# One pool of four PSUM banks for scores and shared tiles, single-bank refill, and another order of the last units in a fused attention and gated-feed-forward kernel

## The chip, the cores and the metric

The kernel runs on one core of a Trainium2 chip. Five engines work side by side, each in its own program order, and wait for one another through semaphores: PE (TensorE, matmuls), ACT (ScalarE), DVE (VectorE), POOL (GpSimd) and SP (SyncE, which issues the transfers). Matmuls write to eight accumulation banks of 128 x 512 fp32, called `ps` here. The metric is device time in microseconds (us), the median of several runs.

## The reference, cut to what matters

```
xn  = layernorm(x)                               # x: 1 x 2048 x 512, no scale, no shift
q, k, v = split(xn @ wqkv)                       # 32 heads of width 16
p   = softmax(q k^T / 4)                         # 2048 x 2048 per head
A   = (p v) @ wo
B   = (silu(xn @ w1) * (xn @ w3)) @ w2           # inner width 1792
out = x + A + B
```

Nearly all work of the attention is one element per score: 32 x 2048 x 2048 scores that are formed, whose row maximum is subtracted, that go through the exponential, and that meet v.

## The kernel before, in words

The heads are taken in 8 groups of four (one head on 32 rows of the PE array), the queries in 4 chunks of 512. A chunk and a group give two **units** of 256 queries; the last pair gives three, of 256, 128 and 128, so there are 65 units.

Each unit forms its scores twice. **Stage 1** (`p1_cand`, matmul L772) lays 128 queries against 512 keys for two heads into two banks; DVE takes the row maximum of both (L793, 128x1024), and when all of a unit's are there, L834 joins them into `negm`, the negated maximum. There are 1024 such steps, on bank pairs 0-1 and 2-3 in turn. POOL writes the negated maximum into `Z` (L810, L812); it reaches two spare rows of `QT` by two transfers, or, for the first unit and the last three (FAST_AUG), by a new projection of the queries with `Z` added (`tile_QT2`, evacuated by ACT at L602). **Stage 2** (`p2_cand`, matmul L888) then forms the transposed scores less the maximum, 512 columns (a bank) at a time, and ACT takes the exponential straight out of the bank (L905). There are 2048 such exponentials, in banks 4, 5 and 6 in a fixed rotation: number n goes to bank 4 + n mod 3.

Everything else shares **bank 7**, one tile at a time: the projections KT, QT and V, the product of weights and v (`tile_PV`, evacuated as `U` at L969), the feed-forward's gate and up tiles (L641, L643, L647), and the output tiles (L704). At the end the feed-forward part of the last outputs is set aside (`tile_OUTA`, L716), and once the last unit's attention is there, `tile_OUTB` adds the attention part (L729) in banks 0 to 3. All of these are column matmuls issued by one helper, L453. The last three units (FAST_PV) get their softmax sum by extra matmuls against ones, and DVE divides (L958, L960); the others go through a chain of transfers and POOL (L992, L1014).

The order of all instructions is fixed when the kernel is built. A planner keeps its own estimate of when each engine is free, and again and again emits the earliest candidate. `pick_pe` weighs three candidates for PE: a stage-1 step (a), a stage-2 step (b), a column matmul (c). Where there is no column matmul to do, `fill_cand` offers a **fill**: four matmuls of the identity against xnT into a free bank, whose result nobody reads (in the profile `ps<-xnT,ident`). It does so where the columns that the planner counted in the last `LOAD_WIN` = 2.3 us are under `LOAD_MIN` = 12000, between the 48th stage-1 step and the last one. `assign` gives banks to tiles; `choose` says which tile is next; `pv_ready` lets a PV tile start when at most 6 of its unit's exponentials are still to be emitted.

Of the kernel before, what the change touches and what calls it, by code (L numbers as in the profile page):

```python
# [225 lines left out]
def _build(nc, A_x, A_wqkv, A_wo, B_w1, B_w3, B_w2, out):  # L226
# [15 lines left out]
    STARVE = 0.7  # L242
    COUP = 0.1
    PACE = 4500
    PACE_CAP = 6000
    LAG = 44
    LOAD_WIN = 2.3
    LOAD_MIN = 12000

    units = []  # L250
    for qc in range(NQC):
# [4 lines left out]
    NU = len(units)  # L256
# [4 lines left out]
    P = _Prog()  # L261
# [4 lines left out]
    with ctx:  # L266
# [342 lines left out]
        def ffn_from(sc, fc):  # L609
            last = sc == NQC - 1  # L610
            lo = sc * CHUNK + (100 if sc else 40)
            hi = (sc + 1) * CHUNK + (-24 if last else LAG)
            return lo + (hi - lo) * fc // FC

        def ffn_pair(sc, fc):
# [230 lines left out]
        p2_n = [0]  # L846
        exp_n = [0]
        exp_unit = [0] * NU
        pt_free = list(range(NT, NPT))
        pt_slot = {}  # L850
        exp_emitted = set()

        def p2_cand():
# [1 line left out]
            if u >= NU or ("AUG", u) not in done or not pt_free:  # L855
                return None
            n = p2_n[0]
            if exp_n[0] < n - 2:
                return None
            b = 4 + n % 3  # L860
            if b in bank_tenant:
                return None
            qc, g, q0, nq = units[u]
            kpb = 512 // nq
# [17 lines left out]
            def emit():  # L882
                rest.pop(best[1])
                pt_free.pop(0)

                def f(e):
                    for i in range(kpb):
                        ins = e.matmul(bank(b)[:, i * nq:(i + 1) * nq],  # L888
                                       KT[32 * j:32 * j + 32, g, (k0 + i) * 128:(k0 + i + 1) * 128],
                                       QT[32 * j:32 * j + 32, qs, q0:q0 + nq],  # L890
                                       start=True, stop=True, tile_position=(32 * j, 0))
                    return ins
                P.pe(f, reads, writes, "row", (j,), kpb * _c_mm(nq), name="p2_%d" % n, first="act")
                note_load(st, 512)
                p2_n[0] += 1
                pt_slot[(u, kb, j)] = sl
                if not rest:
                    p2_u[0] += 1
                    p2_units_done[0] = p2_u[0]

                def cb(op):
                    exp_n[0] += 1
                    exp_unit[u] += 1
                    exp_emitted.add((u, kb, j))
                expq.append(_Item(lambda e: e.activation(PT[:, sl, :], bank(b), ACTF.Exp, scale=SCALE),  # L905
                                  [("ps", b)], [("PT", sl)], _c_act(512), cb=cb))
# [137 lines left out]
        def pv_ready():  # L1044
            u = pv_u[0]
            if u >= NU:
                return False
            left = len(p2_list[u]) - exp_unit[u]
            if left > 6:
                return False  # L1050
            if u in FAST_PV:
                return True
            return u < NUB or u_live[0] < NUB
# [29 lines left out]
        def assign():  # L1083
            if head_tiles or not (0 in pvlog or ("AUG", 0) in done):
                for bk in (7, 6, 5, 4):
                    if bk in bank_tenant or (bk != 7 and p2_n[0] > 0):
                        continue
                    for k, t in enumerate(head_tiles):
                        if ok(t):
                            give(head_tiles.pop(k), bk)  # L1090
                            break
            if 7 not in bank_tenant and not head_tiles:
                t = choose()
                if t is not None:
                    give(t, 7)
            if ("AUG", 0) not in done and p1_n[0] > 0 and not head_tiles:
                for bk in (6, 5, 4):
                    if bk not in bank_tenant and p2_n[0] == 0:
                        if crit and ok(crit[0]):
                            give(crit.pop(0), bk)  # L1100
            if red_n[0] >= NP1:
                for bk in (0, 1, 2, 3):
                    if bk not in bank_tenant and tail_outs and ok(tail_outs[0]):
                        give(tail_outs.pop(0), bk)
        pvlog = set()

        def col_cand():
            best = None
            for t in active:
                if not t.groups:  # L1110
                    continue
                g = t.groups[0]
# [37 lines left out]
            return st, emit, dur  # L1150

        couple = [-1.0]
        loadlog = []

        def note_load(st, w):
# [5 lines left out]
            return sum(w for t, w in loadlog if t >= st - LOAD_WIN) < LOAD_MIN  # L1161

        def fill_cand():
            if head_tiles or p1_n[0] < 48 or p1_n[0] >= NP1 or not low_load(P.free["pe"]):
                return None
            st = None
            for fb in (7, 4 + p2_n[0] % 3):
                if fb in bank_tenant or (fb != 7 and (exp_n[0] < p2_n[0] - 2 or p2_n[0] == 0)):
                    continue
                s_ = P.pe_start("col", None, P.ready("pe", (), [("ps", fb)]))  # L1170
                if st is None or s_ < st - 0.05:
# [10 lines left out]
            return st, emit, _c_mm(512)  # L1182
        n_fill = [0]

        def pick_pe():
            a = p1_cand()
            b = p2_cand()
# [6 lines left out]
                a[1]()  # L1194
            if b is not None and b[0] <= couple[0] + 0.12:
                return b[0], b[1]
            if c is None:
                if a is not None and (b is None or a[0] <= b[0] + COUP):
                    return a[0], go_a
                return None if b is None else (b[0], b[1])  # L1200
            if a is not None and a[2] <= end + 0.02:
                return a[0], go_a
            starving = (b is not None and b[2] <= max(end, c[0]) + 0.02 and not expq
                        and P.free["act"] < b[0] + STARVE)
            if a is None or c[0] + c[2] <= a[2] + TOL:
                if starving:
                    return b[0], b[1]
# [163 lines left out]
```

## Time and profile before

| what | value |
|---|---|
| median of 3 runs | 1308.74 us (1305.94 to 1310.98) |
| profiled execution: its time, its span | 1309.81 us, 1308.0 us |
| granted PE clock, mean over the span | 0.967 |
| busy: ACT, DVE, PE | 1223.6, 1199.7, 1194.0 us |
| 1024 row maxima on DVE (L793) | 1175.8 us busy |
| 2048 exponentials on ACT (L905) | 1084.4 us busy |
| fills on PE | 1528 matmuls, 131.0 us |
| the last row maximum ends | 1224.2 us |
| the last exponential ends | 1301.9 us |

The time is taken outside the program, the span from the first to the last instruction of the profiled execution. A busy engine is not always at its best pace: an instruction that comes alone is counted with its whole duration, while one that follows closely on another overlaps with it. So the mean spacing within a run of equal instructions tells more than the share of busy time.

### The profile page before, as it was taken

What the parts mean: (1) busy time and instruction counts of PE and PEld (TensorE: products, weight loads), DVE (VectorE), ACT (ScalarE), POOL (GpSimd) and SP (SyncE); (2) the same over time, 40 slices, a digit from 0 to 9 for tenths busy, and PEclk for the clock granted to TensorE, in tenths of its full rate; (3) what the DMA queues carried; (4) which work ended last, traced back from release to release, by engine and by line L of the source; (5) the groups of instructions that cost most, each with busy time, mean ns of one, the idle gap of its engine ahead of it and who ended that gap; (6) DMA issues with size and microseconds to landing.
All of it is one profiled execution on the core that took longest, in us unless ns stands there. A gap on an engine that the chain in (4) does not pass through costs nothing.

```text
span 1308.0 us, 39060 instructions
## 1 busy us (share of the span) xinstructions
PE 1194.0 (91%) x16785; PEld 439.0 (34%) x16785; DVE 1199.7 (92%) x1141; ACT 1223.6 (94%) x2413; POOL 357.6 (27%) x453
## 2 busy tenths in 40 slices
PE   5999899889999999999999999999999988899997
PEld 2323333333333333333333333333333333333334
DVE  6889999999999999999999999999999999999402
ACT  5689999999999999999999999999999999999984
POOL 4012332222321233323331133333331143443110
PEclk8979999999899999899999999999999999999985
DMA  7001100101010111111101111111101121110000
GB/s 217 3 14 24 27 18 17 25 18 25 18 21 22 34 26 25 25 26 27 25 16 27 34 27 24 25 26 27 23 18 27 23 44 33 35 24 9 5 5 18
DMA packets 112844, 36.24 MB, mean 28 GB/s; under 512 B 98232, under 2 KB 112672, under 8 KB 112672
## 3 DMA queue, kind: packets, MB, share of 16 engines
q1 hardware_dynamic: 112672, 33.76, 12.0%
q8 instruction: 131, 2.15, 0.7%
q14 instruction: 41, 0.34, 0.1%
HBM read 22.81 MB, written 2.10 MB: 19 GB/s over the span
## 4 chain that ended last, share of the span: by engine, by line
PE 52%; ACT 40%; DVE 4%; issue 2%; DMA 1%; SPq 0%
ACT PT L905 30%; PE ps L453 28%; PE ps L888 15%; PE ps L772 8%; DVE part L793 4%; ACT th L641 2%; ACT zg L643 2%; ACT ub L647 2%; ACT U L969 1%; ACT KT L536 1%; ACT QT L579 1%; DMA hT<-in_A_wqkv_dram 1%; ACT osb L704 0%; ACT osb L491 0%; DVE R L958 0%
## 5 line engine op out<-in xcount | busy, mean ns | idle before, releaser
L793 DVE TENSOR_REDUCE part<-ps 128x2 f32<-128x1024 f32 x1024 | 1175.8, 1216 | 28.6 <-PE ps L772 17.0
L905 ACT ACTIVATE PT<-ps 128x512 bf16<-128x512 f32 x2048 | 1084.4, 619 | 50.5 <-PE ps L888 34.2
L888 PE MATMUL ps<-QT,KT 32*128 32x256 bf16 (+1 forms) x4160 | 577.7, 276 | 20.6 <-ACT PT L905 9.6
L772 PE MATMUL ps<-KT,QT 32*128 32x512 bf16 x2048 | 444.4, 387 | 5.2 <-DVE part L793 4.3
L888 PEld LDWEIGHTS ps<-QT,KT 32*128 32x128 bf16 x4160 | 188.6, 93 | 312.6 <-ACT PT L905 235.2
L992 POOL TENSOR_TENSOR Rc<-Lc,mone 128x8 f32<-128x8 f32 x62 | 101.5, 1637 | 390.6 <-DMA Lc<-U 390.6
L453 PE MATMUL ps<-PT,Vaug 128*17 128x256 bf16 (+1 forms) x4160 | 178.8, 279 | 14.1 <-ACT zg L643 2.4
L453 PE MATMUL ps<-xnT,w 128*32 128x512 bf16 x1792 | 142.0, 390 | 32.9 <-ACT zg L643 22.5
L772 PEld LDWEIGHTS ps<-KT,QT 32*128 32x128 bf16 x2048 | 114.8, 91 | 160.6 <-issue 96.6
L453 PE MATMUL ps<-xnT,ident 128*32 128x512 bf16 x1528 | 131.0, 391 | 2.4
L453 PEld LDWEIGHTS ps<-PT,Vaug 128*17 128x17 bf16 x4160 | 83.2, 91 | 98.4 <-issue 60.6
L628 POOL TENSOR_TENSOR a<-zg,ub 128x512 f32<-128x512 bf16 x56 | 64.7, 1155 | 126.1 <-ACT ub L647 126.1
L810 POOL TENSOR_SCALAR Z<-negm 128x8 bf16<-128x8 f32 x64 | 14.7, 229 | 210.2 <-DVE negm L834 210.2
L630 POOL TENSOR_TENSOR hT<-a,t 128x512 bf16<-128x512 f32 x56 | 71.1, 1270 | 3.1
L453 PEld LDWEIGHTS ps<-xnT,w 128*32 128x32 bf16 x1792 | 37.1, 95 | 98.8 <-issue 83.1
L453 PE MATMUL ps<-w,hT 128*32 128x512 bf16 x896 | 70.3, 384 | 0.0
L958 DVE RECIPROCAL R<-ps 128x128 f32<-128x128 f32 (+1 forms) x3 | 3.7, 1224 | 71.3 <-PE ps L453 71.3
L453 PEld LDWEIGHTS ps<-xnT,ident 128*32 128x32 bf16 x1528 | 31.1, 94 | 59.0 <-issue 39.1
L453 PE MATMUL ps<-xnT,wk_on 128*32 128x512 bf16 x512 | 42.2, 406 | 7.0 <-ACT KT L536 4.9
L626 POOL TENSOR_SCALAR t<-th 128x512 f32<-128x512 bf16 x56 | 34.9, 623 | 49.9 <-ACT th L641 49.8
L453 PE MATMUL ps<-xnT,wq 128*32 128x512 bf16 (+2 forms) x576 | 41.8, 369 | 7.2 <-ACT U L969 2.5
L1014 POOL TENSOR_TENSOR on_b<-U,R 128x256 bf16<-128x256 f32 x32 | 23.3, 728 | 56.6 <-DMA R<-Rrow 56.6
(75 smaller groups left out, 458.7 us busy)
## 6 DMA issues: line engine op xcount, KB each, us to landing
w<-in_B_w_dram SPq DMA_DIRECT2D x112, 128.0 KB
R<-Rrow SPq DMA_DIRECT2D x248, 16.0 KB
PT<-in_A_x_dram SPq DMA_DIRECT2D x4, 512.0 KB
xr<-in_A_x_dram SPq DMA_DIRECT2D x16, 128.0 KB
out_dram<-osb SPq DMA_DIRECT2D x16, 128.0 KB
QT<-Zs SPq DMA_DIRECT2D x122, 2.0 KB
w<-in_B_w_dram SPq DMA_DIRECT2D x1, 1792.0 KB
hT<-in_A_wqkv_dram SPq DMA_DIRECT2D x3, 512.0 KB
```

The lines of the kernel that those rows point to most:

```text
L453: ins = e.matmul(bank(bk)[32 * i:32 * i + m, c0:c0 + ncols], make_lhsT(i), rhs_ap(i), start=start, stop=stop, tile_position=(0, 32 * i), **kw)
L626: q.append(_Item(lambda e: e.tensor_scalar(t1[:, :], th[:, ss, :], 1.0, 1.0, ALU.mult, ALU.add), [("th", ss)], [("t1",)], 0.62, 0.72))
L628: q.append(_Item(lambda e: e.tensor_tensor(a32[:, :], zg[:, ss, :], ub[:, ss, :], ALU.mult), [("zg", ss), ("ub", ss)], [("a32",)], 1.1, 1.25))
L630: q.append(_Item(lambda e: e.tensor_tensor(hT[:, fc, :], a32[:, :], t1[:, :], ALU.mult), [("a32",), ("t1",)], [("hT", fc)], 1.25, 1.35, cb ...
L641: return [_Item(lambda e: e.activation(th[:, ss, :], bank(bk), ACTF.Tanh, scale=0.5), [("ps", bk)], [("th", ss)], _c_act(512), cb=part_don ...
L643: _Item(lambda e: e.activation(zg[:, ss, :], bank(bk), ACTF.Identity, scale=0.5), [("ps", bk)], [("zg", ss)], _c_act(512), cb=part_done, n ...
L647: return [_Item(lambda e: e.activation(ub[:, ss, :], bank(bk), ACTF.Identity), [("ps", bk)], [("ub", ss)], _c_act(512), cb=part_done)]
L772: ins = e.matmul(bank(2 * sl + i), QT[32 * j:32 * j + 32, qs, q * 128:(q + 1) * 128], KT[32 * j:32 * j + 32, g, kc * 512:(kc + 1) * 512], ...
L793: redq.append(_Item(lambda e: e.tensor_reduce(part[:, par, qt, 2 * pair:2 * pair + 2, kc], ps[:, sl * 1024:(sl + 1) * 1024].rearrange("p ( ...
L888: ins = e.matmul(bank(b)[:, i * nq:(i + 1) * nq], KT[32 * j:32 * j + 32, g, (k0 + i) * 128:(k0 + i + 1) * 128], QT[32 * j:32 * j + 32, qs, ...
L905: expq.append(_Item(lambda e: e.activation(PT[:, sl, :], bank(b), ACTF.Exp, scale=SCALE), [("ps", b)], [("PT", sl)], _c_act(512), cb=cb))
L992: poolq["nrm"].append(_Item(lambda e: e.tensor_tensor(Rc[:, pp, 0:nl], Lc[:, pp, 0:nl], mone[:, 0:nl], ALU.pow), [("Lc", pp), ("mone",)], ...
```

## The change

- The banks 7, 6, 5, 4 are one pool (`pool_banks`). `free_bank` takes the pool's bank that comes free first. A stage-2 step takes any free bank instead of the next in rotation, at most four being in flight (`p2_busy`); the wait for the exponential two steps earlier is gone. Once all row maxima are done, banks 0 to 3 join the pool.
- A shared tile takes any free bank of the pool, at most one such tile at a time until the row maxima are done, at most five after.
- A fill may go into any free bank of the pool, and fills are offered until the last PV tile has begun, not only up to the last stage-1 step. `LOAD_MIN` goes from 12000 to 12500.
- A PV tile starts when at most 4 exponentials of its unit are still to be emitted. The last chunk's feed-forward is due 24 stage-1 steps earlier (-48 for -24). Among several tiles that wait, QT2 goes first and OUTB last (`rank`).
- After the last stage-1 step, `pick_pe` issues stage-2 steps in runs (`tail_run`: begun when no exponential is queued, ended when three are, or when the next has to wait). Before it, a stage-2 step also goes ahead of a column matmul where the next unit's maxima are ready (`behind`) and ACT would soon be idle.

Core of the diff (parts left out are marked):

```diff
-    LOAD_MIN = 12000
+    LOAD_MIN = 12500
...
-            hi = (sc + 1) * CHUNK + (-24 if last else LAG)
+            hi = (sc + 1) * CHUNK + (-48 if last else LAG)
...
+        def pool_banks():
+            return POOL_BANKS if red_n[0] < NP1 else POOL_BANKS + (3, 2, 1, 0)
+
+        def free_bank():
+            best = (None, 0.0)
+            for b in pool_banks():
+                if b in bank_tenant or b in p2_busy:
+                    continue
+                r = P.ready("pe", (), [("ps", b)])
+                if best[0] is None or r < best[1] - 1e-6:
+                    best = (b, r)
+            return best
...
-            if exp_n[0] < n - 2:
-                return None
-            b = 4 + n % 3
-            if b in bank_tenant:
+            b, b_rd = free_bank()
+            if b is None or len(p2_busy) >= 4:
                 return None
...
-            if left > 6:
+            if left > 4:
...
-            if 7 not in bank_tenant and not head_tiles:
-                t = choose()
+            if not head_tiles and sum(b in bank_tenant for b in pool_banks()) < (1 if red_n[0] < NP1 else 5):
+                bk = free_bank()[0]
+                t = None if bk is None else choose()
                 if t is not None:
-                    give(t, 7)
+                    give(t, bk)
...
-            if head_tiles or p1_n[0] < 48 or p1_n[0] >= NP1 or not low_load(P.free["pe"]):
+            if head_tiles or p1_n[0] < 48 or pv_u[0] >= NU or not low_load(P.free["pe"]):
...
-            for fb in (7, 4 + p2_n[0] % 3):
-                if fb in bank_tenant or (fb != 7 and (exp_n[0] < p2_n[0] - 2 or p2_n[0] == 0)):
+            for fb in pool_banks():
+                if fb in bank_tenant or fb in p2_busy:
                     continue
...
+            if p1_n[0] >= NP1 and b is not None:
+                if len(expq) <= TAIL_LOW:
+                    tail_run[0] = True
+                if len(expq) >= TAIL_HIGH or b[2] > end + 0.12:
+                    tail_run[0] = False
+                if tail_run[0] or c is None:
+                    return b[0], b[1]
+                if b[2] <= end + 0.12 or c[0] + c[2] <= b[2] + 0.4:
+                    return c[0], c[1]
...
-            starving = (b is not None and b[2] <= max(end, c[0]) + 0.02 and not expq
-                        and P.free["act"] < b[0] + STARVE)
+            starving = (b is not None and b[2] <= max(end, c[0]) + 0.02
+                        and ((not expq and P.free["act"] < b[0] + STARVE) or (behind() and
+                             P.free["act"] + 0.476 * len(expq) < b[0] + STARVE)))
```

More of the change, by code (lines that the diff above doesn't have):

```diff
@@ L246, in _build @@
     LAG = 44
+    POOL_BANKS = (7, 6, 5, 4)
+    TAIL_LOW = 0
+    TAIL_HIGH = 3
     LOAD_WIN = 2.3
-    LOAD_MIN = 12000
+    LOAD_MIN = 12500
     units = []
@@ L848, in _build @@
         exp_unit = [0] * NU
+        p2_busy = set()
+        def pool_banks():
[9 more added lines that the diff above has]
+            return best
         pt_free = list(range(NT, NPT))
@@ L884, in emit @@
                 pt_free.pop(0)
+                p2_busy.add(b)
                 def f(e):
@@ L901, in cb @@
                 def cb(op):
+                    p2_busy.discard(b)
                     exp_n[0] += 1
@@ L1085, in assign @@
                 for bk in (7, 6, 5, 4):
-                    if bk in bank_tenant or (bk != 7 and p2_n[0] > 0):
+                    if bk in bank_tenant or bk in p2_busy or (bk != 7 and p2_n[0] > 0):
                         continue
@@ L1100, in assign, with rank @@
                             give(crit.pop(0), bk)
[L1101 to L1104, printed above, removed]
+            if red_n[0] >= NP1 and tail_outs and ok(tail_outs[0]):
+                bk = free_bank()[0]
+                if bk is not None:
+                    give(tail_outs.pop(0), bk)
         pvlog = set()
+        def rank(t):
+            return 0 if t.name.startswith("QT2") else 2 if t.name.startswith("OUTB") else 1
         def col_cand():
             best = None
-            for t in active:
+            for t in sorted(active, key=rank):
                 if not t.groups:
@@ L1152, in _build @@
         couple = [-1.0]
+        tail_run = [False]
         loadlog = []
@@ L1183, in _build, with behind @@
         n_fill = [0]
+        def behind():
+            return ("AUG", min(p2_u[0] + 1, NU - 1)) in done
         def pick_pe():
```

## The prediction, made before the result was known

> **What bounds the kernel now.** I read the busy times first, then the chain of waits, then the stretches of the span one by one, since the shares of busy time (PE 91%, DVE 92%, ACT 94%) name no engine. The windows, cut at the places where the work changes (length, then busy time and instructions of each engine, then PEclk, the granted clock):
>
> ```profile
> PE 1194.0 (91%) x16785; PEld 439.0 (34%) x16785; DVE 1199.7 (92%) x1141; ACT 1223.6 (94%) x2413; POOL 357.6 (27%) x453
> 0.00:64.00 64.00, 48.01 (x597) 18.72 (x599) 46.52 (x69) 37.52 (x65) 16.05 (x35) 0.92 0.41 112
> 80.00:96.00 16.00, 15.05 (x156) 4.81 (x156) 11.19 (x11) 10.93 (x22) 4.96 (x6) 0.52 0.01 2
> 96.00:1216.00 1120.00, 1033.50 (x14784) 377.52 (x14784) 1110.37 (x1027) 1092.89 (x2178) 328.59 (x402) 0.99 0.12 25
> 352.00:360.00 8.00, 7.70 (x96) 2.56 (x92) 6.26 (x8) 5.88 (x12) 0.48 (x3) 0.61 0.04 9
> 532.00:540.00 8.00, 8.00 (x73) 2.35 (x72) 7.00 (x7) 7.07 (x15) 2.65 (x3) 0.57 0.07 10
> 1224.00:1263.00 39.00, 37.51 (x452) 12.60 (x448) 0.72 (x4) 36.55 (x69) 4.74 (x4) 1.00 0.03 4
> 1263.00:1302.00 39.00, 36.12 (x516) 17.88 (x516) 5.41 (x7) 22.55 (x40) 0.73 (x1) 0.50 0.05 13
> ```
>
> There are three regimes. In the body, 96 to 1216, DVE is busy for 1110.4 of 1120 us: the row maxima set the pace. The tail, behind the last maximum, has no DVE work to speak of: 39 us at full clock, then 39 us at half. In the head, to 64 us, every engine waits. ACT's 1092.9 us in the body look full but are not, as its exponentials show:
>
> ```profile
> L905 ACT ACTIVATE PT<-ps 128x512 bf16<-128x512 f32 x2048 | 1084.4, 619 | 50.5 <-PE ps L888 34.2
> 96.00:1216.00 1120.00, 994.89 (x1890) 0.99 0.12 25
> 838.91 6.91 ACT PT L905 x14
> 1216.18 8.02 DVE L793 TENSOR_REDUCE part<-ps 128x2 f32<-128x1024 f32 x7
> 1225.15 9.69 ACT L905 ACTIVATE PT<-ps 128x512 bf16<-128x512 f32 x15
> 1268.43 0.60 ACT L905 ACTIVATE PT<-ps 128x512 bf16<-128x512 f32 x1 [0.48 <-PE ps L888]
> 1269.50 0.60 ACT L905 ACTIVATE PT<-ps 128x512 bf16<-128x512 f32 x1 [0.48 <-PE ps L888]
> 1301.33 0.60 ACT L905 ACTIVATE PT<-ps 128x512 bf16<-128x512 f32 x1 [0.26 <-PE ps L888]
> ```
>
> The second row is the body again, L905 alone: 994.89/1890 = 0.526 us for one exponential. Fed without a gap, 14 of them take 6.91 us, 0.49 us each. The last row maximum ends at 1216.18 + 8.02 = 1224.2. ACT could give back 1890 x 0.036 = 68 us in the body, beside its 27 us of open idle. In the tail ACT is not the limit at all: 0.646 us for one at full clock (9.69/15), 1.07 us at half (1268.43 to 1269.50, waiting for PE each time). PE's alternation sets that:
>
> ```profile
> 1230.57 0.39 PE L888 MATMUL ps<-QT,KT 32*128 32x256 bf16 x2
> 1230.88 0.40 PE L453 MATMUL ps<-wo,wk_on 128*32 128x512 bf16 x4
> 1231.21 0.39 PE L888 MATMUL ps<-QT,KT 32*128 32x256 bf16 x2
> 1259.75 3.50 PE L888 MATMUL ps<-QT,KT 32*128 32x256 bf16 x14 [0.26 <-ACT PT L905]
> 1260.00:1264.00 4.00, 3.38 (x32) 1.22 (x32) 0.00 (x0) 4.00 (x9) 1.51 (x1) 0.85 0.02 1
> 1264.00:1268.00 4.00, 4.00 (x44) 1.04 (x36) 0.00 (x0) 1.90 (x4) 0.00 (x0) 0.50 0.12 21
> ```
>
> Two stage-2 matmuls (one exponential) and four column matmuls take 0.64 us. That is 2560 columns, 13,600 in 3.4 us (the time of three row maxima), and the clock stays full. At 1259.75 PE has stage 2 alone, 14 x 256 = 3584 columns in 3.5 us, and the clock halves for good.
>
> **Part 1: exponentials leave the tail.** Place one is PE around the last stage-1 step (`KT,QT` 128x512); `QT,KT` is stage 2, `wo,wk_on` an output tile, `xnT,wq` with `ident,Z` the last unit's QT2. Before:
>
> ```order
> L772 MATMUL ps<-KT,QT 128x512 x2
> L888 MATMUL ps<-QT,KT 128x256 x4
> L453 MATMUL ps<-w,hT 32x512 x4
> L888 MATMUL ps<-QT,KT 128x256 x2
> L453 MATMUL ps<-wo,wk_on 32x512 x8
> L453 MATMUL ps<-xnT,wq 32x128 x16
> ```
>
> Now:
>
> ```order
> L775 MATMUL ps<-KT,QT 128x512 x2
> L904 MATMUL ps<-QT,KT 128x256 x4
> L456 MATMUL ps<-PT,Vaug 17x256 x20
> L904 MATMUL ps<-QT,KT 128x256 x2
> L456 MATMUL ps<-PT,Vaug 17x256 x20
> L456 MATMUL ps<-wo,wk_on 32x512 x4
> L904 MATMUL ps<-QT,KT 128x256 x6
> ```
>
> Counted over the whole order, 102 exponentials stand behind that last step before, 60 now; the feed-forward's output matmuls (`w,hT`, 60 of them before) have left the tail too, and stage 2 comes in sixes instead of twos. At the full-clock pace 42 exponentials are 42 x 0.646 = **27.1 us less tail**. They are done in the body instead, 42 x 0.49 = 20.6 us of ACT, under DVE's row maxima: 68 + 27 us of room cover it. Without that cover the 20.6 us come back.
>
> **Part 2: the clock of the tail.** Place two is PE near the end, now (`xnT,ident` is a fill; the earlier kernel has none here, only alternations of four stage-2 matmuls and Vaug/ones groups):
>
> ```order
> L904 MATMUL ps<-QT,KT 128x128 x12
> L456 MATMUL ps<-xnT,ident 32x512 x4
> L456 MATMUL ps<-wo,wk_on 32x512 x4
> L456 MATMUL ps<-xnT,ident 32x512 x8
> L904 MATMUL ps<-QT,KT 128x128 x32
> L456 MATMUL ps<-xnT,ident 32x512 x24
> L904 MATMUL ps<-QT,KT 128x128 x8
> ```
>
> There are 56 fill matmuls behind the last maximum, where there were none. If the clock holds, the half-clock stretch's 40 exponentials take 40 x 0.646 = 26 us for 39: **13 us less**. Runs of stage 2 save some switches, down to ACT's 0.49 at best (a further 9 us over 60); I take none of that as certain. The fills cost 14 groups of four at 0.215 us (1.03 us for 16, below) = 3.0 us. So the tail, 1308.0 - 1224.2 = 83.8 us, becomes 83.8 - 27.1 - 13 + 3 = 46.7; for the longer runs I take off 2: **45 us**. Bounds: ACT alone, 60 x 0.49 + 6.1 us from the last exponential (1301.93) to the end + 1 = 36.5; all at half clock, 60 x 1.07 + 6.1 = 70.
>
> **Part 3: the head.** Place three is PE's first work (`hT,xnT` is V, whose weights come by the last transfer). Before, then now:
>
> ```order
> L515 MATMUL ps<-ident,osb 128x128 x16
> L453 MATMUL ps<-hT,xnT 32x512 x16
> L453 MATMUL ps<-xnT,wk_on 32x512 x16
> L453 MATMUL ps<-xnT,wq 32x512 x16
> L453 MATMUL ps<-hT,xnT 32x512 x16
> L772 MATMUL ps<-KT,QT 128x512 x4
> ```
>
> ```order
> L518 MATMUL ps<-ident,osb 128x128 x16
> L456 MATMUL ps<-xnT,wk_on 32x512 x16
> L456 MATMUL ps<-xnT,wq 32x512 x16
> L456 MATMUL ps<-hT,xnT 32x512 x16
> L775 MATMUL ps<-KT,QT 128x512 x4
> ```
>
> ```profile
> 13.80 1.90 PE L453 MATMUL ps<-hT,xnT 128*32 128x512 bf16 x16 [1.58 <-DMA hT<-in_A_wqkv_dram]
> 17.92 1.03 PE L453 MATMUL ps<-hT,xnT 128*32 128x512 bf16 x16
> 19.31 2.36 DVE L793 TENSOR_REDUCE part<-ps 128x2 f32<-128x1024 f32 x2 [0.74 <-PE ps L772]
> 32.20 4.62 DVE L793 TENSOR_REDUCE part<-ps 128x2 f32<-128x1024 f32 x4 [4.88 <-PE ps L772]
> 41.76 9.14 DVE L793 TENSOR_REDUCE part<-ps 128x2 f32<-128x1024 f32 x8 [4.94 <-PE ps L772]
> ```
>
> K no longer stands behind a V that waits 1.58 us for its transfer, and further V tiles move behind later K tiles. DVE waits there for 0.74, 4.88 and 4.94 us (and two gaps between). The first start cannot gain more than the 0.74; the others depend on K tiles that wait for normalised rows from ACT, so I take **2.5 us** (0 to 6). The first exponential comes after 22 stage-1 steps, not 27, so ACT starts with a lead.
>
> **Part 4: the body's clock.** With 12500 there are 148 more fill matmuls before the last maximum: 37 x 0.215 = 8 us of PE, under its 1120 - 1033.5 = 86 us idle; 8 us if not covered. Three half-clock stretches cost DVE 4.8 us (80:96), 1.7 and 1.0. Summing the order's columns over three stage-1 steps, the early one stands where 6,100 to 10,800 columns are planned; now no place there has under 14,800. Later, 7 places before and 6 now have under 12,300. So the early stretch goes, **4.8 us**, and the two short ones may come back elsewhere (bounds 0 to 7.5).
>
> The single-bank refill itself (no rotation; four in flight where no shared tile holds a bank) I cost at nothing in the body: DVE's pace hides it. It is what brings the 42 exponentials forward.
>
> **Sum.** Last maximum at 1224.2 - 2.5 - 4.8 = 1216.9; with the 45 us tail a span of 1261.9. The profiled execution's time is 1.8 above its span, and 1.1 above the median: 1262.6, so **1263 us**.
>
> **Rivals.** (a) ACT becomes the bound of the body: the 42 exponentials collide with evacuations and DVE waits. For it: only 27 us of open idle. Against: spacing 0.526 where 0.49 is possible. Price 20.6 us: 1284. Chance 0.12.
>
> (b) The tail's clock halves all the same. For it: in the order, 12 stage-2 matmuls, one fill group, an output group, two fill groups and 32 more of stage 2 are 13,800 columns for 11 exponentials, which ACT takes 5.4 us for: 8,700 in 3.4 us, far below the 13,600 that held. Against: 24 fills follow at once. If half clock holds from the start, 60 x (1.07 - 0.646) = 25: 1288; for the last 20 alone, 8: 1271, which is inside the forecast. Chance of the large one 0.13; of (a) and (b) together 0.02, 1309, no change.
>
> (c) Slower: stage 2 through any of four banks starves PE in the body more often and the clock drops in and out. Place: the body; price: 1.7 and 1.0 us of DVE in the windows at 352 and 532, whose clock of 0.61 and 0.57 means 6 to 7 of 8 us at half, so 0.15 to 0.27 per us. It outweighs the gain of 46 us from 46/0.25 = 184 us at half clock on; at 300 us the time is 1263 + 75 = 1338. Against it, rotation through three banks kept PEclk at 0.99 over 1120 us, and the change adds fills. Chance 0.04. The Trainium skill, in "TensorE: Matmul & The Clock Gate", section "A second HAM failure mode: psum-queue depth-cycling", describes this: cycling through banks lets PE idle for moments often enough that the clock swings, and throughput falls. By that rule the price of (c) would be the likely result; the trace of before does not bear it out.
>
> That the change does nothing is excluded where it is a matter of order (102 against 60).
>
> **How the numbers follow.** Forecast 0.69, 1250 to 1276: tail 36.5 to 55, head and clock 2 to 13 us, whose far ends (1248 and 1278) need all at once. With (a) and (b) on the far side, 1250 to 1288 holds 8 in 10. A difference under 0.5% cannot be told from none. Faster 0.69 + 0.12 + 0.13 = 0.94, same 0.02, slower 0.04.
>
> **What would show it.** Last row maximum at 1214 to 1220; PEclk 1.0 through most of the tail; last exponential about 39 us behind the last maximum; exponentials in the body spaced 0.51 us; no half clock near 80. It is wrong if DVE's busy share in the body falls below 98%, or if the tail takes over 55 us.

## The result, and the profile after

The changed kernel takes 1257.93 us (median; 1251.74 to 1261.56), against 1309.68 us for the kernel before: ratio 0.9604, 95% interval 0.956 to 0.965. The forecast was 1263, range 1250 to 1288. The profiled execution took 1256.76 us, with a span of 1255.0.

The changed kernel's page, then its windows in the same columns as before:

```profile
PE 1171.5 (93%) x16989; PEld 431.4 (34%) x16989; DVE 1200.6 (96%) x1141; ACT 1203.5 (96%) x2413; POOL 358.7 (29%) x453
L796 DVE TENSOR_REDUCE part<-ps 128x2 f32<-128x1024 f32 x1024 | 1176.7, 1216 | 18.4 <-PE ps L775 10.1 <-PE ps L904 3.6
L922 ACT ACTIVATE PT<-ps 128x512 bf16<-128x512 f32 x2048 | 1068.7, 636 | 24.8 <-PE ps L904 14.7 <-PE ps L775 1.6
L904 PE MATMUL ps<-QT,KT 32*128 32x256 bf16 (+1 forms) x4160 | 565.1, 272 | 16.2 <-ACT QT L582 0.7 <-ACT PT L922 0.6
```

```profile
0.00:64.00 64.00, 49.72 (x603) 19.04 (x603) 50.46 (x73) 43.32 (x79) 16.10 (x35) 0.95 0.41 112
80.00:96.00 16.00, 15.49 (x232) 5.57 (x224) 15.93 (x16) 15.91 (x34) 3.90 (x6) 1.00 0.14 27
96.00:1216.00 1120.00, 1061.16 (x15170) 385.26 (x15166) 1110.82 (x1030) 1098.11 (x2212) 333.21 (x406) 0.99 0.12 25
1215.00:1251.00 36.00, 30.51 (x788) 16.17 (x784) 7.06 (x12) 30.67 (x61) 3.10 (x3) 0.97 0.07 17
```

In the body DVE still sets the pace (1110.8 of 1120 us). The half-clock stretch at 80 is gone. Above all, the stretch behind the last row maximum, whose second half ran at half clock before, now runs at 0.97. DVE's last row maximum and the exponentials behind it, from the timeline:

```profile
1213.95 1.23 DVE L796 TENSOR_REDUCE part<-ps 128x2 f32<-128x1024 f32 x1 [0.50 <-PE ps L904]
1218.56 17.53 ACT L922 ACTIVATE PT<-ps 128x512 bf16<-128x512 f32 x33
1237.51 5.66 ACT L922 ACTIVATE PT<-ps 128x512 bf16<-128x512 f32 x11 [1.43 <-PE ps L904]
1243.82 5.50 ACT L922 ACTIVATE PT<-ps 128x512 bf16<-128x512 f32 x11 [0.65 <-PE ps L904]
```

The last maximum ends at 1215.2 (1224.2 before) and the span 39.8 us later (83.8 before). So of the 53.0 us that the span lost, 9.0 were lost up to the last maximum and 44.0 behind it. In the tail 33 exponentials come at 17.53/33 = 0.53 us, where they took 0.65 and then 1.07. The chain of waits says the same: ACT's exponentials are now 39% of it (30% before), and PE falls from 52% to 49%.

All runs are summed up below. "Last max" is the end of the last row maximum, "tail" what follows it to the end of the span, "in tail" the exponentials that start behind it, "half clock" the time at a granted clock of 0.5 from 60 us to the last maximum, and behind it: all from the one profiled execution. The ratio is to the kernel before, run on the same chip in the same session.

| kernel | median us | ratio (95%) | last max | tail | in tail | half clock |
|---|---|---|---|---|---|---|
| before | 1309.7 | 1 | 1224.2 | 83.8 | 100 | 30.7, 45.2 |
| changed | 1257.9 | 0.960 (0.956 to 0.965) | 1215.2 | 39.8 | 58 | 12.1, 5.7 |
| before, look-ahead alone | 1312.3 | 1.005 (1.002 to 1.009) | 1244.8 | 66.8 | 58 | 65.0, 47.8 |
| changed, rotation instead of pool | 1275.0 | 0.975 (0.970 to 0.981) | 1229.5 | 44.0 | 62 | 27.3, 6.8 |
| changed, no fills in the tail | 1260.1 | 0.963 (0.957 to 0.969) | 1217.5 | 42.8 | 58 | 13.9, 22.3 |
| changed, no look-ahead | 1262.5 | 0.966 (0.960 to 0.971) | 1209.5 | 50.2 | 75 | 7.2, 9.2 |
| changed, more fills | 1255.1 | 0.961 (0.959 to 0.963) | 1212.4 | 40.5 | 60 | 0, 3.2 |
| changed, extra work on ACT | 1293.2 | 0.990 (0.985 to 0.994) | 1252.0 | 39.6 | 57 | 47.9, 7.5 |
| changed, head as before | 1265.1 | 0.968 (0.966 to 0.970) | 1225.4 | 39.4 | 57 | 23.8, 5.6 |
| rotation and more fills | 1272.5 | 0.973 (0.969 to 0.977) | 1232.5 | 41.5 | 61 | 27.3, 3.0 |
| changed, no runs in the tail | 1266.7 | 0.968 (0.966 to 0.971) | 1213.5 | 51.0 | 58 | 12.1, 18.6 |
| before, runs alone | 1291.5 | 0.987 (0.984 to 0.990) | 1223.4 | 67.5 | 100 | 23.8, 30.8 |
| changed, extra work planned for | 1295.3 | 0.982 (0.975 to 0.988) | 1228.7 | 47.0 | 72 | 54.6, 3.3 |
| changed, more fills, costed reciprocals | 1252.7 | 0.958 (0.955 to 0.960) | 1212.2 | 38.8 | 60 | 0, 4.7 |

The time of one kernel moves with the granted clock of the run (its mean over the span). The changed kernel took 1251.74 us at 0.995 and 1261.56 at 0.983, and the kernel before took 1305.8 to 1307.9 us at 0.973 in all three sessions of the experiments. So rows that lie near each other are also compared at like clocks below. The ratio of the row "extra work planned for" rests on its two faster runs, while its median takes in two slow ones (1300.45 and 1309.70 us, at clocks of 0.949 and 0.939).

### The profile page after: what moved, and what is told of

Read it like the earlier page. It is cut to its first block, busy times and chain, and to the rows that moved or that the text cites. A ratio compares the mean times of both kernels' runs of the same rounds, so it can differ in the third digit from the quotient of the medians.

```text
span 1255.0 us, 39328 instructions
## 1 busy us (share of the span) xinstructions
PE 1171.5 (93%) x16989; PEld 431.4 (34%) x16989; DVE 1200.6 (96%) x1141; ACT 1203.5 (96%) x2413; POOL 358.7 (29%) x453
## 4 chain that ended last, share of the span: by engine, by line
PE 49%; ACT 48%; issue 1%; DVE 1%; DMA 1%; SPq 0%; ACTq 0%; POOL 0%
ACT PT L922 39%; PE ps L456 28%; PE ps L904 12%; PE ps L775 8%; ACT th L644 2%; ACT zg L646 2%; ACT ub L650 2%; ACT QT L582 1%; ACT KT L539 1%; DMA PT<-in_A_x_dram 1%; ACT U L986 1%; DVE part L796 0%; ACT osb L494 0%; ACT osb L707 0%; DVE R L975 0%
## 5 line engine op out<-in xcount | busy, mean ns | idle before, releaser
L922 ACT ACTIVATE PT<-ps 128x512 bf16<-128x512 f32 x2048 | 1068.7, 636 | 24.8 <-PE ps L904 14.7
L904 PE MATMUL ps<-QT,KT 32*128 32x256 bf16 (+1 forms) x4160 | 565.1, 272 | 16.2 <-ACT QT L582 0.7
L775 PE MATMUL ps<-KT,QT 32*128 32x512 bf16 x2048 | 433.4, 385 | 2.0 <-DVE part L796 1.5
L904 PEld LDWEIGHTS ps<-QT,KT 32*128 32x128 bf16 x4160 | 182.1, 92 | 292.7 <-ACT PT L922 184.8
L775 PEld LDWEIGHTS ps<-KT,QT 32*128 32x128 bf16 x2048 | 111.2, 91 | 145.4 <-issue 94.7
L456 PE MATMUL ps<-xnT,ident 128*32 128x512 bf16 x1732 | 138.8, 385 | 10.9 <-DVE osb L732 0.2
L456 PEld LDWEIGHTS ps<-xnT,ident 128*32 128x32 bf16 x1732 | 34.5, 94 | 83.3 <-ACT PT L922 70.1
L1031 POOL TENSOR_TENSOR wk_on<-U,R 128x256 bf16<-128x256 f32 x30 | 21.9, 728 | 70.2 <-DMA R<-Rrow 69.9
```

Of the source, the lines that this page charges most:

```text
L456: ins = e.matmul(bank(bk)[32 * i:32 * i + m, c0:c0 + ncols], make_lhsT(i), rhs_ap(i), start=start, stop=stop, tile_position=(0, 32 * i), **kw)
L775: ins = e.matmul(bank(2 * sl + i), QT[32 * j:32 * j + 32, qs, q * 128:(q + 1) * 128], KT[32 * j:32 * j + 32, g, kc * 512:(kc + 1) * 512], ...
L904: ins = e.matmul(bank(b)[:, i * nq:(i + 1) * nq], KT[32 * j:32 * j + 32, g, (k0 + i) * 128:(k0 + i + 1) * 128], QT[32 * j:32 * j + 32, qs, ...
L1031: poolq["nrm"].append(_Item(lambda e: e.tensor_tensor(onorm[ob][:, g, q0:q0 + nq], U[:, us, 0:nq], R[:, pp, 0:nq], ALU.mult), [("U", us)] ...
```

## The experiments

**1. The look-ahead alone.** The orders of two variants show what the prediction had not looked at: the changed kernel with the pool undone still leaves 62 exponentials behind the last stage-1 step, and the kernel before with `behind()` alone leaves 60. So the look-ahead by itself moves the order forward; the refill of single banks is not needed for it. The look-ahead is not needed either for a good part of it: the changed kernel without it leaves 76 (experiment 4), so the rest of the change brings 26 of the 42 forward on its own. The first run puts it alone into the kernel before:

```diff
-            starving = (... and not expq and P.free["act"] < b[0] + STARVE)
+            starving = (... and ((not expq and P.free["act"] < b[0] + STARVE) or (behind() and
+                             P.free["act"] + 0.476 * len(expq) < b[0] + STARVE)))
```

> The kernel before plus the look-ahead alone: a stage-2 step may go ahead of a column matmul where the next unit's maxima are ready and ACT would soon be idle. No pool, no single-bank refill, no fills in the tail. Its order has 60 exponentials behind the last stage-1 step (102 before), but only 1092 fill matmuls (1528 before) and 30 places with under 12,300 columns in three stage-1 steps (7 before). Theory A (the tail is shortened by whatever lets exponentials run ahead of the row maxima, here the look-ahead; the body's pace stays DVE's): 42 exponentials x 0.646 = 27 us leave the tail, whose second half still runs at half clock; more half-clock stretches in the body cost 2 to 8 us: 1284 to 1290. Theory B (the prediction's: the single-bank refill from a pool brings the exponentials forward, three banks in rotation cannot): ACT waits for banks and DVE for PE, the 20.6 us of exponentials come back in the body: 1300 or more.

Measured: 1312.3 us, 0.5% slower than before. The tail fell by 17.0 us to 66.8, but the last maximum came 20.6 us later. That is the price that the prediction gave to its rival (a), 20.6 us, to the digit by chance: the exponentials left the tail and came back in the body. The body's window (a clock of 0.97), then the groups of the maxima and of stage 2:

```profile
96.00:1200.00 1104.00, 1017.81 (x13939) 365.88 (x13933) 1077.60 (x991) 1069.28 (x2140) 320.76 (x392) 0.97 0.12 25
```

```profile
L793 DVE TENSOR_REDUCE part<-ps 128x2 f32<-128x1024 f32 x1024 | 1182.8, 1220 | 41.3 <-PE ps L772 18.5 <-PE ps L888 16.9
L888 PE MATMUL ps<-QT,KT 32*128 32x256 bf16 (+1 forms) x4160 | 607.2, 279 | 21.7 <-ACT PT L905 10.0 <-DMA QT<-Zs 0.6
```

PE waits 10.0 us for the exponential that frees the next bank in turn (9.6 before, 0.6 in the changed kernel), and DVE's idle time rises from 28.6 to 41.3 us. But the wait for banks is hardly longer than before the look-ahead, and this kernel also has 1092 fills instead of 1528, and 65.0 us of half clock up to the last maximum instead of 30.7. By the changed kernel's own runs (9.8 us more for a mean clock lower by 0.012, which over 1255 us is some 30 us at half clock) those 34 us would cost about 11 us, an estimate. Theory B's time came out; how much of the 20.6 us is the banks and how much the clock, no run separates, for the look-ahead with the old rotation and more fills was not run.

**2. The pool undone.** The changed kernel with stage 2 in rotation over banks 4 to 6 and shared tiles in bank 7, until the last maximum (fills go back to bank 7 and the next bank in rotation, which the cut leaves out):

```diff
-            b, b_rd = free_bank()
-            if b is None or len(p2_busy) >= 4:
+            if exp_n[0] < n - 2:
+                return None
+            b = 4 + n % 3
+            if b in bank_tenant:
                 return None
...
-            return POOL_BANKS if red_n[0] < NP1 else POOL_BANKS + (3, 2, 1, 0)
+            return (7,) if red_n[0] < NP1 else (7, 3, 2, 1, 0)
```

> The changed kernel with the pool undone until the last row maximum: stage 2 in the fixed rotation over banks 4, 5 and 6, shared tiles in bank 7 alone; the look-ahead, the fills in the tail and the tail's order stay. 62 exponentials behind the last stage-1 step, 1384 + 44 fills, 18 low places. Theory A (the pool as such is worth little, the look-ahead does it): within 5 us of the changed kernel, 1256 to 1263, the upper part of it from half-clock stretches in the body. Theory B (the pool brings the exponentials forward): the order cannot be kept, 20 us back: about 1278.

Measured: 1275.0 us, 17 us above the changed kernel, nearer to theory B. The last maximum comes 14.3 us later: 6.2 of it are there by the hundredth maximum (149.2 against 143.0), 8.1 arise behind it; the tail adds 4.2 with four exponentials more in it. PE waits 8.2 us for the exponential ahead of stage-2 matmuls (0.6 with the pool), by the table of waits (us in total, times, longest):

```profile
PE ps L906 <- ACT PT L924: 8.2, 25, 0.6
```

**3. No fills in the tail.**

```diff
-            if head_tiles or p1_n[0] < 48 or pv_u[0] >= NU or not low_load(P.free["pe"]):
+            if head_tiles or p1_n[0] < 48 or p1_n[0] >= NP1 or not low_load(P.free["pe"]):
```

> The changed kernel with fills offered only up to the last stage-1 step, as before: 60 exponentials in the tail, 1676 fills ahead of it, none in it. Theory A (the fills hold the clock): the tail's clock halves where stage 2 runs alone and stays there, some 20 to 30 of the 60 exponentials at 1.07 instead of 0.5 to 0.65 us, less 3 us for fills not done: 1266 to 1276. Rival (runs of stage 2 and dense output tiles hold the clock without fills): 1255 to 1259, PEclk near 1.0 in the tail.

Measured: 1260.1 us. The interval holds the changed kernel's ratio, so by time the fills in the tail are worth nothing that can be told. The trace shows that they do what they are for, and that it hardly matters: 22.3 us of this tail are at half clock, against 5.7, and it is 3.0 us longer. Two windows of it, and ACT's row of the timeline across the second:

```profile
1217.00:1261.00 44.00, 34.92 (x740) 19.23 (x732) 8.35 (x14) 30.89 (x61) 3.09 (x3) 0.73 0.07 17
1248.00:1253.00 5.00, 4.79 (x133) 3.57 (x129) 0.69 (x1) 5.00 (x11) 0.00 (x0) 0.50 0.09 30
```

```profile
1245.22 7.95 ACT L922 ACTIVATE PT<-ps 128x512 bf16<-128x512 f32 x16 [1.40 <-PE ps L904]
```

From 1248 to 1253 PE runs at half clock and ACT is busy all 5.00 us; the 16 exponentials take 0.50 us each. The 1.07 us for one at half clock came where it met the old alternation. Both theories had a wrong half: the clock does halve, and the time does not follow.

**4. No look-ahead.** The changed kernel with the old `starving` condition; the diff is that of experiment 1, reversed.

> The changed kernel without the look-ahead (stage 2 goes first only where no exponential is queued, as before); pool, single-bank refill and tail as changed. 76 exponentials behind the last stage-1 step. Theory A (each exponential left in the tail costs its pace): 16 x 0.49 to 0.65 = 8 to 10 us more: 1266 to 1268. Rival (an exponential in the tail is hidden by PE's other work there): within 3 us of 1258.

Measured: 1262.5 us, 4.6 above the changed kernel (the intervals overlap). The tail is 10.4 us longer for 17 exponentials more in it, 0.6 each, as theory A had it; but the last maximum comes 5.7 us earlier, which neither theory had. So an exponential moved into the body does not look free even with the pool. How much it costs is not pinned down: this order also has 1960 fills ahead of the last maximum instead of 1676. Against the run with more fills (experiment 5, 2364 fills, last maximum at 1212.4) the last maximum is 2.9 us earlier, so some 3 to 6 of the 10.4 us come back in the body, from one execution of each.

**5. More fills.**

```diff
-    LOAD_MIN = 12500
+    LOAD_MIN = 14500
```

> The changed kernel with LOAD_MIN 14500 instead of 12500: 2364 fill matmuls ahead of the last row maximum instead of 1676, 72 instead of 56 behind it; 2 places with under 12,300 columns instead of 6. Theory A (the two half-clock stretches left ahead of the last maximum cost DVE 1 to 1.7 us each, and PE has the time for 172 more groups of four): the last maximum 2 to 3 us earlier, 1254 to 1257. Rival (the extra 37 us of PE delay stage-1 steps): the last maximum later, 1262 or more.

Measured: 1255.1 us. Ahead of the last maximum no half clock is left (12.1 us in the changed kernel), and that maximum comes 2.8 us earlier, as expected; the ratio of 0.961 (0.959 to 0.963) cannot be told from the changed kernel's. What can be seen is the spread: 1254.69 to 1256.46, where the changed kernel went from 1251.74 to 1261.56. The changed kernel's best run is still the faster: at a clock of 0.995 it took 1251.74 us, this kernel 1255.18. The added fills hold the clock; they do not make a run at a like clock faster.

**6. Extra work on ACT, order unchanged.**

```diff
                 def twice(e):
+                    e.activation(junk[:, 0, :], bank(bk)[:, 0:208], ACTF.Identity)
                     return e.activation(ub[:, ss, :], bank(bk), ACTF.Identity)
```

and the same ahead of `th`.

> The changed kernel, its order unchanged, with 112 extra activations of 208 columns on ACT, one ahead of each gate and each up evacuation, into a tile that nobody reads: about 25 us of ACT work, all of it ahead of the last row maximum. Theory A (ACT has room under DVE's pace, as the prediction's cover says): the last maximum at most 3 to 6 us later, 1258 to 1264. Rival (ACT is as good as the bound of the body once the exponentials run ahead): 15 to 25 us more, 1273 to 1283.

Measured: 1293.2 us, 35 us more; the last maximum at 1252.0, 36.8 us later. The rival was nearer, and even it was too low. The tail kept its 39.6 us. The two new groups count their overlapping ends whole; ACT's busy time in all rises by 27.4 us, from 1203.5 to 1230.9. The new groups, DVE's and stage 2's waits:

```profile
L655 ACT ACTIVATE junk<-ps 128x208 bf16<-128x208 f32 x56 | 22.1, 395 | 0.1
L646 ACT ACTIVATE junk<-ps 128x208 bf16<-128x208 f32 x56 | 21.0, 374 | 0.1
L803 DVE TENSOR_REDUCE part<-ps 128x2 f32<-128x1024 f32 x1024 | 1184.9, 1217 | 47.0 <-PE ps L911 22.7 <-PE ps L782 18.0
L911 PE MATMUL ps<-QT,KT 32*128 32x256 bf16 (+1 forms) x4160 | 574.3, 275 | 22.0 <-ACT ub L656 6.5 <-ACT PT L929 1.5 <-ACT QT L583 0.7
```

DVE now waits 22.7 us at places where stage 2 stands ahead of stage 1 on PE (3.6 in the changed kernel), and stage 2 waits for the bank of the up tile that ACT emptied late (6.5 us). There are also 47.9 us of half clock up to the last maximum. At like clocks the loss is about the work that was added: 1285.87 us at 0.986, where the changed kernel took 1259.10 at 0.988 and 1261.56 at 0.983. So in this order the body has no room left on ACT: it has two limits, DVE's maxima and ACT's share, tied together by PE's fixed order.

**7. The head as before.**

```diff
+            if not head_tiles and p2_n[0] == 0 and 7 not in bank_tenant:
+                t = choose()
+                if t is not None:
+                    give(t, 7)
```

> The changed kernel with the head's order of before: until the first exponential a V tile may start in bank 7 beside the head's own tiles, so that V stands ahead of the first K tile again. 60 exponentials behind the last stage-1 step as in the changed kernel. Theory A (the prediction's: K ahead of V gains 2.5 us, 0 to 6): the hundredth row maximum 2 to 6 us later than the changed kernel's 143.0, 1260 to 1264. Rival (the head is bound by ACT and the transfers whatever PE's order): 1256 to 1259, the hundredth at 143 to 144.

Measured: 1265.1 us, 7.2 above the changed kernel, with the hundredth maximum at 150.3 instead of 143.0. PE's first column matmuls and DVE's first maxima in the changed kernel, then DVE's in this one:

```profile
13.47 1.90 PE L456 MATMUL ps<-xnT,wk_on 128*32 128x512 bf16 x16 [0.79 <-ACT xnT L524]
19.15 2.36 DVE L796 TENSOR_REDUCE part<-ps 128x2 f32<-128x1024 f32 x2 [0.19 <-PE ps L775]
33.20 14.80 DVE L796 TENSOR_REDUCE part<-ps 128x2 f32<-128x1024 f32 x13 [7.31 <-PE ps L775]
```

```profile
31.77 4.62 DVE L796 TENSOR_REDUCE part<-ps 128x2 f32<-128x1024 f32 x4 [4.94 <-PE ps L775]
41.33 10.27 DVE L796 TENSOR_REDUCE part<-ps 128x2 f32<-128x1024 f32 x9 [4.94 <-PE ps L775]
```

With V ahead there are two waits of 4.94 us, as before the change; with K ahead one of 7.31, then no stop. By the sixteenth maximum that is 3.6 us (50.5 against 46.9); by the hundredth 7.3, with a half-clock stretch of 6.8 us from 95 to 102 in this kernel and none near it in the changed one. So all that the change gained up to the last maximum, 9.0 us, is there by the hundredth (10.3 us).

**8. The rotation with more fills.** Experiment 2 with LOAD_MIN 14500.

> The kernel of the second run (fixed rotation over three banks, shared tiles in bank 7) with LOAD_MIN 14500: 1968 + 64 fill matmuls instead of 1384 + 44. It tells the clock from the banks: that run's last row maximum came 14.3 us later than the changed kernel's, with 17 us more at half clock, and 6 us of it were there by the hundredth maximum. Theory A (the half clock makes the rest): the last maximum 5 to 8 us earlier, about 1267. Theory B (PE waits for ACT to free the next bank in turn; fills cannot help): within 3 us of 1275, PE still waiting 8 us for exponentials ahead of stage-2 matmuls.

Measured: 1272.5 us, within 3 us of experiment 2, with the last maximum 3.0 us later in the trace and as much half clock (27.3 us). The median is theory B's time; its mechanism came only in part, for PE's wait ahead of stage 2 fell to 1.6 us while DVE's did not (31.4 us against 28.8).

The profiled execution is the slowest of four, though: they go from 1264.09 us at a clock of 0.997 to 1275.76 at 0.984. At like clocks the rotation lies 9.4 us above the pool with more fills (1254.69 us at 0.996, experiment 5), and experiment 2 lies 13.3 us above the changed kernel (1274.81 at 0.984, 1261.56 at 0.983). Of these, 6.2 us lie ahead of the hundredth maximum in both pairs, and 1.0 and 4.2 in the tail. That leaves 2 to 3 us for the rest of the body, an estimate, since head and tail are from the profiled executions. So most of the 8.1 us that experiment 2 lost behind the hundredth maximum goes with the clock, and little is left for waits for a bank.

**9. No runs in the tail.** The block that begins with `if p1_n[0] >= NP1 and b is not None` is taken out of `pick_pe`.

> The changed kernel without the rule that issues stage 2 in runs once the row maxima are done (the old alternation of one exponential and one or two column groups is back). 60 exponentials behind the last stage-1 step, 1676 fills ahead of it and, since column matmuls are now always at hand, none behind it. The run without fills in the tail had a tail of 42.8 us with 22 us of it at half clock, so fills are worth little; the run with the look-ahead alone had as many exponentials in a tail of 66.8 us. Theory C (the runs are what makes the tail short, since one exponential per alternation at half clock costs 1.07 us): tail 60 to 66 us, 1277 to 1284. Theory A (the prediction's: the exponentials that left are most of it, and only the clock comes on top): tail 45 to 50, 1263 to 1268.

Measured: 1266.7 us, within theory A's range; tail 51.0, just above it and far from theory C's. The runs are worth something all the same. Against the run without fills in the tail (experiment 3, which has none either) the tail is 8.2 us longer, with less half clock (18.6 against 22.3 us). At full clock (1.00 in the window of each row) its exponentials come at 22.18/35 = 0.63 us, where the changed kernel's came at 0.53:

```profile
1217.85 22.18 ACT L922 ACTIVATE PT<-ps 128x512 bf16<-128x512 f32 x35
```

PE at half clock in this kernel, then ACT beside it:

```profile
1244.09 0.60 PE L904 MATMUL ps<-QT,KT 32*128 32x128 bf16 x4
1244.62 0.29 PE L456 MATMUL ps<-PT,Vaug 128*17 128x128 bf16 x4
1244.69 0.32 PE L456 MATMUL ps<-PT,ones_t 128*32 128x128 bf16 x4
1244.95 0.60 PE L904 MATMUL ps<-QT,KT 32*128 32x128 bf16 x4
```

```profile
1244.73 0.60 ACT L922 ACTIVATE PT<-ps 128x512 bf16<-128x512 f32 x1 [0.26 <-PE ps L904]
1245.59 0.60 ACT L922 ACTIVATE PT<-ps 128x512 bf16<-128x512 f32 x1 [0.26 <-PE ps L904]
```

One exponential for each alternation, 0.86 us apart, though the column work between is only two short groups. In the changed kernel two exponentials share one alternation of 1.1 us (here at full clock; for runs at half clock experiment 3 showed 0.50 us for one):

```profile
1230.18 0.41 PE L904 MATMUL ps<-QT,KT 32*128 32x128 bf16 x8
1231.28 0.41 PE L904 MATMUL ps<-QT,KT 32*128 32x128 bf16 x8
1232.38 0.41 PE L904 MATMUL ps<-QT,KT 32*128 32x128 bf16 x8
```

**10. The runs alone.** The block of experiment 9 put into the kernel before, and nothing else.

> The kernel before plus that rule alone: 102 exponentials behind the last stage-1 step as before, 1528 fills ahead of it, none behind it. The last row maximum stays at 1224. Theory C: runs at 0.5 to 0.6 us for one exponential make the tail 57 to 66 us instead of 83.8: 1283 to 1291. Theory A: the tail stays within 8 us of 83.8, 1298 to 1309, since the exponentials are still there and the clock halves.

Measured: 1291.5 us, tail 67.5 instead of 83.8, with all 102 exponentials still behind the last stage-1 step and no fill: theory C, just past the upper end of its ranges. The last maximum stays (1223.4). Two rows of its tail. In both the exponentials come at about 0.50 us, though the clock is half from 1249.9 to 1260.2, which is most of the first row, and 0.93 in the window of the second:

```profile
1246.12 11.89 ACT L907 ACTIVATE PT<-ps 128x512 bf16<-128x512 f32 x24
1264.35 3.04 ACT L907 ACTIVATE PT<-ps 128x512 bf16<-128x512 f32 x6 [0.25 <-PE ps L890]
```

**11. Extra work that the planner counts.** Experiment 6 with 0.225 us added to the planner's cost of the two evacuations.

> The kernel with 112 extra activations on ACT (some 25 us), but now the planner counts them, so the order is another: 73 exponentials behind the last stage-1 step instead of 60, 22 low places instead of 6. The run whose planner did not know of them took 35 us more. Theory D (that time was ACT late against an order fixed beforehand, which holds up PE and, behind it, stage 1; ACT itself has room): the last maximum within 8 us of the changed kernel's 1215.2, and 13 more exponentials in the tail cost 6 to 7 us: 1264 to 1274. Rival (ACT is the bound of the body): the whole 25 us come through, 1280 to 1290.

Measured: 1295.3 us, but from 1277.5 to 1309.7 in four runs, at clocks from 0.975 down to 0.939; the profiled one, the fastest, has the last maximum 13.5 us later than the changed kernel and 54.6 us of half clock. Its order has 22 low places. The rival's time fits the median, but with that much half clock the median does not separate ACT's room from the clock. At like clocks there is an answer in part: 1277.51 us at 0.975, where experiment 6 took 1293.41 at 0.976. An order planned for the extra work gets 16 us back, so ACT does have some room in another order. How much of the 25 us is left is open, since the changed kernel has no run at that clock.

**12. More fills and costed reciprocals.** In the changed kernel's tail PE waits behind an output group for the first reciprocal, and ACT behind PE:

```profile
1234.26 1.76 DVE L975 RECIPROCAL R<-ps 128x256 f32<-128x256 f32 x1 [18.47 <-PE ps L456]
1236.54 0.61 PE L456 MATMUL ps<-wo,wk_on 128*32 128x512 bf16 x8 [1.56 <-DVE wk_on L977]
```

```diff
-    LOAD_MIN = 12500
+    LOAD_MIN = 14500
...
-                                  [("R", u % 2, j_) for j_ in range(4)], _c_dve(nq)),
+                                  [("R", u % 2, j_) for j_ in range(4)], 1.76 if nq == 256 else 0.96),
```

> The changed kernel with LOAD_MIN 14500 and with the planner's cost for the reciprocals of the last units set to what the trace shows, 1.76 us for 256 columns and 0.96 for 128: the changed kernel's trace has PE waiting 1.56 us behind an output group for the first of them, and ACT 1.43 us behind PE. 62 exponentials and 52 fills in the tail. Expected: the run with 14500 alone (1255.1) less 1 to 2 us, 1252 to 1255. Rival (the wait only moves to the next output group): 1255 to 1257.

Measured: 1252.74 us (1252.14 to 1253.02), ratio 0.958 (0.955 to 0.960). PE's wait for the first product of the reciprocal falls from 1.56 to 0.35 us. The tail is 38.8 us, and its last 25 exponentials come without a stop:

```profile
1234.24 0.40 PE L456 MATMUL ps<-wo,wk_on 128*32 128x512 bf16 x4 [0.35 <-DVE wk_on L977]
1232.28 13.05 ACT L922 ACTIVATE PT<-ps 128x512 bf16<-128x512 f32 x25 [0.15 <-PE ps L904]
```

The expectation held: at a clock of 0.996 this kernel took 1253.02 us, and experiment 5 1254.69 and 1255.06. Against the changed kernel the medians are 5 us apart and the traces 4.0, but the intervals of the ratios overlap, and the changed kernel's best run (1251.74 us at 0.995) is no slower.

## Why the prediction was right, and where it was not

The sign, the size and the split between body and tail were right: last maximum at 1215.2 where 1216.9 was forecast, tail 39.8 where 45 was, PEclk near full through most of the tail, no half clock near 80, DVE's share of the body at 99%. Two signs came out a little differently: the last exponential ends 34 us behind the last maximum (39 forecast), and the body's exponentials are spaced 0.52 us (0.51 forecast).

That the sum for the tail came so near is in part luck, for its terms missed in both directions. The tails of the table split the 44.0 us that it lost. From before to the look-ahead alone, 42 exponentials fewer, 17.0 us (27.1 forecast). From there to the changed kernel without runs, 15.8 us: this is the rest of the tail's order, in which the feed-forward's output matmuls have left the tail (56 start behind the last maximum in experiment 1, none in experiment 9), more banks are free and 29 us less is at half clock. The runs, 8.2 us (2 forecast). The fills, 3.0 us (13 forecast for the clock that they were to hold, less 3 for themselves). The 15.8 us are not taken apart by any run: the earlier feed-forward was never tried alone. Step by step:

- **Exponentials leave the tail (27.1 us).** The count, 102 to 60, held, and the price of 0.65 us each in the tail was about right where the tail ran near full clock (experiment 4: 0.6). In the kernel before it was too high: 17.0 us for 42 are 0.40 each (experiment 1). It is not a net price: in experiment 4 some 3 to 6 of 10.4 us are paid in the body.
- **"It is what brings the 42 exponentials forward"**, of the single-bank refill, failed as stated. The look-ahead alone does it too (60 left), and the rest of the change without the look-ahead brings 26 of the 42. What differs is what the body then carries: alone the look-ahead costs 20.6 us up to the last maximum (by the estimate of experiment 1, about 11 of them go with the clock); with the whole change 33 more exponentials fit into the same stretch, at 0.521 us each instead of 0.526. The rows for 160 to 1200 us, exponentials alone, before and changed:

```profile
160.00:1200.00 1040.00, 924.96 (x1758) 0.99 0.12 25
```

```profile
160.00:1200.00 1040.00, 932.45 (x1791) 1.00 0.12 25
```

- **The cover ("68 + 27 us of room")** was mis-sized. The room was there for the 42 exponentials, and then used up: 25 us more on ACT came out as 35 us (experiment 6), and as about 25 at like clocks. ACT's smallest spacing of 0.49 us is not room that can be had while PE's order is fixed and each late bank holds up a stage-1 step behind it. "I cost at nothing in the body", of the refill, was nearly right: taking it away costs 8.1 us of body in the traces, but 2 to 3 at like clocks (estimate of experiment 8), beside 6.2 in the head.
- **The tail's clock (13 us from fills, less 3).** The clock held, as forecast, but the 13 us were put down to the wrong part: half clock is 18.6 us instead of 45.2 without any fill or run in the tail (experiment 9), and without the fills alone the tail is 3.0 us longer. The runs of stage 2, for which the prediction took 2 us, are worth 8.2 us in the changed kernel (experiment 9 against 3) and 16.3 us on their own (experiment 10). The step treated pace as a matter of the clock; the runs show that the alternation sets it too, 0.63 us for one against 0.53 at full clock (experiment 9).
- **The head (2.5 us) and the early half clock (4.8 us).** 10.3 us by the hundredth maximum (153.3 to 143.0), 4.0 of them by the sixteenth. The mechanism held, and undoing K ahead of V gave back 7.3; it was somewhat under-sized.
- **Rivals.** (a) came for the look-ahead alone. In the changed kernel it did not (DVE at 99%), and the pool is not shown to be what kept it away: the look-ahead without the pool, but with the rest, loses 8.1 us of body and not 20.6 (experiment 2). (b) did not come. Experiment 3, with 22.3 of 42.8 us at half clock, shows 3.0 us for it where the prediction had 8 for the last 20 exponentials, because the runs stand with it; a tail wholly at half clock, the price of 25 us, was not run. (c) did not come: PEclk in the body went from 0.99 to 1.00 between 96 and 1200. The Trainium skill, in "TensorE: Matmul & The Clock Gate", section "A second HAM failure mode: psum-queue depth-cycling", tells of a kernel in which cycling through banks made the clock swing. That spoke for (c), and these traces do not bear it out: the wider pool cut PE's waits for a bank from 9.6 to 0.6 us, and it is the rotation over three banks that has more half clock (27.3 us against 12.1, one execution of each).

What is left open: what in the rest of the tail's order makes the 15.8 us, how much of the look-ahead's 20.6 us is the clock (experiment 1), and how much room ACT has in an order planned for it (experiment 11).

## What to carry to other kernels

When work is moved from a tail into a body that "has room", ask what ties the engines there: the moved work can come back in the body. Here the look-ahead alone took 17.0 us off the tail and lost 0.5% in all, while the same change without the look-ahead, or without the pool, kept more than half of the gain (1262.5 and 1275.0 us). Where PE feeds another engine by switching between two kinds of matmul, count the switches before the clock: two or more pieces for each switch kept ACT fed even at half clock. Extra matmuls that only hold the clock gained nothing here that can be told in the median, but the spread over four runs was narrower with more of them (9.8 us to 1.8). And where runs of one kernel differ in granted clock, compare two kernels at like clocks before putting a difference down to waits.

## What the runs showed of the hardware that was not expected

- Half clock cost almost no time where PE was not what ACT waited for. With stage 2 in runs, exponentials kept 0.50 us at a granted clock of 0.50 (experiment 3, 1248 to 1253), where the alternation gave 1.07.
- A reciprocal of 128x256 on DVE took 1.76 us, and of 128x128 0.96, against 0.42 and 0.29 us for the multiplication of the same tiles right behind; about five times what the planner assumed (0.34 and 0.20), and enough to stall PE for 1.56 us.
- With the order unchanged, 25 us of extra ACT work came with 36 us more half clock up to the last maximum (47.9 against 12.1, one execution of each; mean clocks of 0.969 to 0.986 in four runs against 0.983 to 0.995), and the loss of 35 us was larger than the work. At like clocks it was about the work.
